# Signing complex gradient sums on TensorE in an S4 channel loop, and moving one copy to VectorE

## The chip, the cores and the metric

The kernel runs on one core of one Trainium2 chip. The metric is the time of one execution in microseconds on the device; the time before is the median of three runs. The engines are TensorE (PE, its weight loads are PEld), VectorE (DVE), ScalarE (ACT), GpSimd (POOL) and SyncE (SP, which issues transfers).

## The reference

The reference is the forward pass and the whole gradient of a gated mix: `out = g * a + (1 - g) * b`, where `a` is multi-head attention over `x` (2048 tokens, 576 channels, 32 heads), `b` an S4 convolution and `g` a sigmoid gate per token. Cut to what this change touches, the S4 part is

```python
dt = exp(log_dt)[:, None];  A = A_re + 1j*A_im;  Bc = B_re + 1j*B_im;  Cc = C_re + 1j*C_im
P = exp((dt*A)[:, :, None] * arange(L))          # 576 channels x 128 states x 2048 steps
K = einsum("dn,dnl,dn->dl", Cc, P, dt*Bc).real   # one filter of 2048 taps per channel
y = irfft(rfft(pad(u)) * rfft(pad(K)))[:L] + u*Dskip
_out, vjp = jax.vjp(forward, ...);  grads = vjp(grad_out)
```

The gradients for `A`, `B`, `C` and `log_dt` need, per channel and state, complex sums over pairs of block states: products (a_r + i a_i)(h_r + i h_i) added up, so that the real part is rr - ii and the imaginary part ri + ir.

## The kernel before

The kernel has a projection stage, then a long attention stage (forward and backward, up to about 2080 us), then the channel loop of the S4 part (up to about 2531 us), and a final stage that forms the outputs. The change lies in the channel loop.

The loop runs over 18 blocks (`NBLK`) of 32 channels (`CB`); the 128 states lie on the partitions. The 2048 tokens are 16 blocks of 128 (`NB`; `NS` = 15). The loop is a software pipeline written out by hand: iteration `i` finishes block `i`, starts the scan of block `i+1`, prepares the inputs of block `i+2` (`sb`) and loads for block `i+3` (`mb`). The order on PE, ACT, DVE and POOL is the order in which the code calls the steps.

The steps of one iteration, with the names that the profile shows:

- `scan`: DVE runs two recurrences in turn, the second half of block `i` and the first half of block `i+1`. Each step is a product `tz` (L733), an addition of `UV` (L736) and an addition into `HG` (L738). `scan_open` (L714) opens a block: it allocates `HG` and copies the first states out of `UV`.
- `rw1` and `rw2`: DVE makes `wab` (L753) and `Rw` (L758) from `HG`.
- `m_sum`, `m_fin`, `m_part`: PE sums `skw` into `misc`, ACT copies into `RX` (L652 to L654); PE makes `psM`, ACT copies it to `mst` (L628), from where it goes to memory.
- `turn_e`: PE transposes `E1n` (1 MB per half block, loaded from memory) into `etp`, ACT copies it to `E1e` (L672). Twice a block.
- `k0`: PE makes 64 matmuls of one column (`misc<-wk,E1n`).
- `uv`: PE multiplies `E1e` and `RX` into `uvp`, ACT scales it into `UV` (L708). Twice a block.
- `t0` and `ybp`: PE adds two products into `yp`, the second from `Rw`; ACT copies `yp` to `yd` (L806).
- `pairs1` and `pairs2`: DVE multiplies `UV` with the casts `hR` and `gR` of `HG` into the bf16 tile `pq` (L812, L841); `psum` lets PE add `pq` over the token blocks with matmuls by the identity into `misc`.
- `m4_copy` (L849): ACT copies the sums from `misc` into the tile `m4` (in the profile `m`), and in the next iteration `sums` (L854, L855) lets POOL subtract and add the four kinds of product into the table `SS`. The last block's `sums` is on DVE.

In a `pq` tile the four kinds of product rr, ri, ir and ii lie side by side, 32 channels each, for every token block. Before, `psum` adds all four in one matmul of 128 columns, 59 matmuls a block (15, 30 and 14 for the three sums). Every matmul has a weight load of its own, also where the weights are the same as before. `etp`, `uvp` and `psM` share four buffers.

Of the kernel before, what the change touches and what calls it, by code (L numbers as in the profile page):

```python
# [9 lines left out]
A = mybir.AluOpType  # L10
ACT = mybir.ActivationFunctionType
BF = mybir.dt.bfloat16
F32 = mybir.dt.float32
# [4 lines left out]
P = 128  # L18


def build(tc, aps, dbg_aps=None, stages=("s1", "attn", "post", "s4", "final")):
    nc = tc.nc
# [6 lines left out]
    def mm(out, lhsT, rhs, start=True, stop=True, **kw):  # L29
        return nc.tensor.matmul(out, lhsT=lhsT, rhs=rhs, start=start, stop=stop, **kw)  # L30
# [31 lines left out]
    with ExitStack() as gctx:  # L62
# [3 lines left out]
        ident_bf = const.tile([P, P], BF, name="ident_bf")  # L66
# [36 lines left out]
        CB = 32  # L103
# [475 lines left out]
        Q = {}  # L579
# [130 lines left out]
        def scan_open(b):  # L710
            B_ = blk(b)
            HG = B_["HG"] = Q["pw"].tile([P, 2, NS, 2, CB], F32, tag="HG", bufs=2, name="HG")
            UVk = B_["UVk"] = B_["UV"][:, :, 0:2 * NB, :].rearrange("p r (s k) c -> p r s k c", s=2)
            (nc.vector.tensor_copy if b == 0 else nc.scalar.copy)(HG[:, :, 0], UVk[:, :, :, 0, :])  # L714

        def scan(*chains):

# [97 lines left out]

        def psum(b, u, pts, n):

            o_ = Q["misc2"][b % 2][:, 4 * u * CB:4 * (u + 1) * CB].rearrange("p (a b c) -> p a b c", a=2, b=2)
            for q, pt_ in enumerate(pts):
                for k in range(n):  # L820
                    mm(o_, lhsT=ident_bf, rhs=pt_[:, :, :, k, :], start=(q == 0 and k == 0),
                       stop=(q == len(pts) - 1 and k == n - 1))

        def pairs1(b):
            B_ = blk(b)
# [16 lines left out]
                                        hR[:, ri, 1:NS, :].unsqueeze(1).to_broadcast([P, 2, NS - 1, CB]), op=A.mult)  # L842
            psum(b, 2, [pD], NS - 1)

        m4s = {}

        def m4_copy(b):
            m4 = m4s[b] = Q["pw"].tile([P, 3, 4, CB], F32, tag="m4", name="m4")
            nc.scalar.copy(m4, Q["misc2"][b % 2][:, 0:12 * CB].rearrange("p (u q c) -> p u q c", u=3, q=4))  # L849

        def sums(b, eng=nc.gpsimd):
            m4 = m4s.pop(b)
            o_ = Q["SS"].rearrange("p (u r) d -> p u r d", r=2)[:, :, :, b * CB:(b + 1) * CB]
            eng.tensor_tensor(o_[:, :, 0], m4[:, :, 0], m4[:, :, 3], op=A.subtract)  # L854
            eng.tensor_tensor(o_[:, :, 1], m4[:, :, 1], m4[:, :, 2], op=A.add)  # L855

        def t0_load(b):
            B_ = blk(b)
# [91 lines left out]
        if "attn" in stages:  # L950
# [5 lines left out]
            with ExitStack() as ctx:  # L956
# [3 lines left out]
                pts = {}  # L960
# [322 lines left out]
                for G in range(NTOT + OFF + 24):  # L1283
# [4 lines left out]
                    if G < NTOT:  # L1288
                        u, s = divmod(G, NST)
                        g, b = units[u]  # L1290
# [11 lines left out]
                    if r1:  # L1302
                        g, b, i, j0 = r1
# [109 lines left out]
        if "s4" in stages:  # L1413
# [8 lines left out]
            with ExitStack() as ctx:  # L1422
# [4 lines left out]
                pps = Q["ps"] = ctx.enter_context(tc.tile_pool(name="s4lps", reuse_waits="tile", bufs=1, space=bass.MemoryType.PSUM))  # L1427
                pidx_i = pc.tile([P, 1], mybir.dt.int32, name="pidx_i")
                nc.gpsimd.iota(pidx_i, pattern=[[0, 1]], base=0, channel_multiplier=1)
                l0col = pc.tile([P, 1], F32, name="l0col")  # L1430
                nc.vector.tensor_copy(l0col, pidx_i)
                l1col = pc.tile([P, 1], F32, name="l1col")
# [17 lines left out]
                with tc.manual_schedule(engines={mybir.EngineType.SP}):  # L1450
                    prep_rx(0, dve_copy)
                    load_en(2, 0, nc.sync.dma_start)
                    wk_cast(0)
                    k0(0)
                    k0_out(0)
                    t0_load(0)
                    turn_e(0, 0, 0, 4, dve_copy)
                    m_sum(0)
                    m_fin(0)
                    uv(0, 0)  # L1460
                    prep_rx(1, dve_copy)
                    load_rx(1, nc.sync.dma_start)
                    turn_e(0, 1, 0, 4, dve_copy)
                    m_part(1)
                    m_skw(1)
                    m_load(2, nc.sync.dma_start)
                    uv(0, 1)
                    turn_e(1, 0, 0, 4, dve_copy)
                    scan_open(0)
                    scan((0, 1, KH, 0), (0, 1, KH, 1))  # L1470
                    turn_e(1, 1, 0, 4)
                    m_sum(1)
                    m_fin(1)
                    load_en(2, 1, nc.sync.dma_start)
                    uv(1, 0)
                    m_part(2)
                    m_skw(2)
                    uv(1, 1)
                    scan_open(1)
                    m_load(3, nc.sync.dma_start)  # L1480
                    prep_rx(2)
                    wk_cast(1)
                    for i in range(NBLK):
                        nx = i + 1 < NBLK
                        mb = i + 3 if i + 3 < NBLK else None
                        sb = i + 2 if i + 2 < NBLK else None
                        if nx:
                            scan((i, KH, NS, None), (i + 1, 1, KH, None))
                        else:
                            scan((i, KH, NS, 0), (i, KH, NS, 1))  # L1490
                        rw1(i)
                        rw2_open(i)
                        rw2(i)
                        if sb is not None:
                            m_sum(sb)
                            m_fin(sb)
                        if mb is not None:
                            m_part(mb)
                            if mb + 1 < NBLK:
                                m_load(mb + 1)  # L1500
                            m_skw(mb)
                        if i > 0:
                            sums(i - 1)
                        if sb is not None:
                            if i % 2 == 1 and (i + 3) // 2 < NBLK // 2:
                                load_par((i + 3) // 2)
                            turn_e(sb, 0, 0, 4)
                        if nx:
                            k0(i + 1)
                        if nx:  # L1510
                            k0_out(i + 1)
                        cast1(i, "hR", 0)
                        nc.scalar.copy(Q["CK"][:, :, :, i * CB:(i + 1) * CB], BK[i]["UV"][:, :, CDK:CDK + 2, :])
                        if sb is not None:
                            uv(sb, 0)
                        t0(i, 0)
                        t0(i, 1)
                        if nx:
                            t0_load(i + 1)
                        cast1(i, "gR", 1)  # L1520
                        if i + 2 >= NBLK:
                            y = 2 * (i + 2 - NBLK)
                            dwq(0, (y, y + 1), "bk", 4)
                            if not nx:
                                dwq_last(0, 1, "bk", 4)
                                load_dq(2)
                        if sb is not None:
                            turn_e(sb, 1, 0, 4)
                        ybp(i, 0)
                        if mb is not None:  # L1530
                            load_en(mb, 0)
                        if sb is not None:
                            uv(sb, 1)
                            scan_open(sb)
                        if i == NBLK - 3:
                            ple_cm.__exit__(None, None, None)
                            Q["nob"] = 2
                            Q["pbw"] = ctx.enter_context(tc.tile_pool(name="pbw0", reuse_waits="tile", bufs=1))
                            r0_cm = tc.tile_pool(name="r0", reuse_waits="tile", bufs=1, side="right")
                            Q["r0"] = r0_cm.__enter__()  # L1540
                            rights.append(r0_cm)
                            load_dq(0)
                        ybp(i, 1)
                        if i == NBLK - 3:
                            load_dq(1)
                        if mb is not None:
                            load_en(mb, 1)
                            prep_rx(mb)
                            if mb % 2 == 1 and mb + 1 < NBLK:
                                load_rx((mb + 1) // 2)  # L1550
                        if mb == NBLK - 1:
                            load_xtok()
                        if sb is None and nx:
                            load_dq(3)
                        yd_out(i, 0)
                        yd_out(i, 1)
                        pairs1(i)
                        pairs2(i)
                        if sb is not None:
                            wk_cast(sb)  # L1560
                        m4_copy(i)
                        if not nx:
                            sums(i, nc.vector)
                        BK.pop(i)

        if "final" in stages and "s4" in stages:
# [304 lines left out]
```

## Time and profile before

| | |
|---|---|
| time before, median of 3 runs | 2687.24 us (2683.43 to 2697.16) |
| the profiled execution's own time | 2685.73 us |
| its span in the profile | 2683.9 us |
| mean granted TensorE clock | 0.968 |
| busy time of PE, DVE, ACT, POOL | 2404.7, 2293.8, 2350.8, 1818.0 us |

Times are microseconds unless marked ns. A busy PE is not PE at its peak, because matmuls overlap and their ends are modelled. From the order of time, the step from one start to the next is the better measure of what a matmul costs in a row of them. "issue" as a releaser means that the engine waited for nothing that the profile shows.

### The profile page before, as it was taken

Reading aid. Unit: us, or ns where it says so; the run is one execution under the profiler, and the core shown is the slowest. Engines: PE = TensorE matmul, PEld = TensorE weight load, DVE = VectorE, ACT = ScalarE, POOL = GpSimd, SP = SyncE. Lnnn points to the kernel's source line nnn. Section 1 sums busy time; section 2 is a strip of 40 time slices with the busy share of each in tenths; the row PEclk is TensorE's granted clock in tenths of the full one; section 3 lists DMA queues with packets and bytes.
Section 4 is the critical chain, followed back from the end, with each engine's and each line's share of the span. In section 5 each row is a group of like instructions: output and inputs, shape, how many; then the busy total and the mean of one; then the engine's idle time right before and its main releaser. Section 6 shows DMA issues by size and latency. Waiting matters only on the chain.

```text
span 2683.9 us, 69949 instructions
## 1 busy us (share of the span) xinstructions
PE 2404.7 (90%) x27411; PEld 1137.9 (42%) x27411; DVE 2293.8 (85%) x4090; ACT 2350.8 (88%) x2744; POOL 1818.0 (68%) x2829
## 2 busy tenths in 40 slices
PE   8799998998899899889888989989887699999999
PEld 4433333333333333333333333333232499998756
DVE  5648999999989999989999989989897589999964
ACT  5489999999999999999999999999995399999221
POOL 0278888888888888888888888887831045555431
PEclk9879999999999999999999999999996699999999
DMA  7637789879979978997898899789679889998895
GB/s 232 196 99 156 154 159 181 167 153 181 172 152 170 183 160 159 178 172 153 165 178 154 161 172 170 153 163 177 143 140 183 191 244 256 259 262 253 261 261 128
DMA packets 1157013, 486.63 MB, mean 181 GB/s; under 512 B 1071061, under 2 KB 1110598, under 8 KB 1154378
## 3 DMA queue, kind: packets, MB, share of 16 engines
q1 hardware_dynamic: 1110650, 341.49, 64.4%
q0 software_dynamic: 44016, 135.16, 18.3%
q10 hardware_dynamic: 2016, 5.51, 0.6%
q8 instruction: 214, 3.51, 0.6%
q14 instruction: 117, 0.96, 0.1%
HBM read 146.27 MB, written 93.80 MB: 89 GB/s over the span
## 4 chain that ended last, share of the span: by engine, by line
ACT 40%; PE 28%; DVE 18%; issue 6%; DMA 4%; POOL 2%; SPq 1%; ACTq 0%; DVEq 0%; POOLq 0%
ACT eb L1387 23%; ACT PT L1382 14%; DVE ds L1392 7%; PE ps_P L30 7%; PE accV L30 2%; PE ps_dx L30 2%; PE turn_p L1095 2%; PE ps_dwq L30 2%; DVE tz L733 2%; PE ps_proj L30 2%; DVE wab L753 2%; PE yp L30 2%; PE accK L30 1%; DVE dvacc L1149 1%; DVE tz L736 1%
## 5 line engine op out<-in xcount | busy, mean ns | idle before, releaser
L1392 DVE TENSOR_TENSOR ds<-ps_P,PT 128x512 bf16<-128x512 f32 x2048 | 1312.3, 683 | 125.5 <-PE ps_P L30 86.8
L1387 ACT ACTIVATE eb<-ps_P 128x1024 bf16<-128x1024 f32 x1024 | 1099.9, 1074 | 34.8 <-PE ps_P L30 34.5
L1382 ACT ACTIVATE PT<-ps_P 128x1024 bf16<-128x1024 f32 x1024 | 1105.0, 1080 | 21.7 <-PE ps_P L30 20.3
L30 PE MATMUL ps_P<-dOaT,VaT_g 32*128 32x512 bf16 x2048 | 581.9, 388 | 31.5 <-DVE ds L1392 16.1
L506 POOL TENSOR_TENSOR et<-eG,eT 128x448 f32<-128x448 f32 x576 | 542.2, 961 | 10.7
L30 PE MATMUL ps_P<-QaT_g,KaT_g 32*128 32x512 bf16 x2048 | 402.9, 386 | 136.5 <-ACT PT L1382 121.8
L30 PE MATMUL ps_P<-KaT_g,QaT_g 32*128 32x512 bf16 x2048 | 406.0, 389 | 1.6 <-ACT eb L1387 0.6
L30 PEld LDWEIGHTS <-KaT_g 32*128 32x128 bf16 x2048 | 147.6, 91 | 467.5 <-issue 451.4
L506 POOL TENSOR_TENSOR Eo<-et,et 128x448 bf16<-128x448 f32 x288 | 327.0, 1135 | 20.8
L30 PEld LDWEIGHTS <-QaT_g 32*128 32x128 bf16 x2048 | 116.1, 91 | 285.3 <-issue 262.4
L30 PE MATMUL accV<-eb,dOa 128*32 128x512 bf16 x2048 | 185.0, 394 | 27.2 <-ACT eb L1387 27.1
L30 PE MATMUL accO<-PT,Vtok_g 128*32 128x512 bf16 x2048 | 207.4, 394 | 0.0
L30 PE MATMUL accK<-dsT,Qtok_g 128*32 128x256 bf16 x4096 | 162.3, 279 | 14.5 <-DMA dsT<-ds 12.4
L30 PE MATMUL accQ<-ds,Ktok_g 128*32 128x512 bf16 x2048 | 161.6, 394 | 2.3 <-DVE dvacc L1149 2.2
L30 PEld LDWEIGHTS <-Vtok_g 128*32 128x32 bf16 x2048 | 52.7, 93 | 222.7 <-issue 222.7
L1100 DVE COPY dsT<-turn_p 128x1024 bf16<-128x1024 bf16 (+1 forms) x216 | 139.2, 644 | 2.1 <-PE turn_p L1095 2.1
L1095 PE MATMUL turn_p<-ident_bf,ds 128*128 128x128 bf16 x1664 | 134.1, 223 | 1.5 <-DVE gb L1167 0.8
L672 ACT COPY E1e<-etp 128x1024 bf16<-128x1024 bf16 x132 | 125.2, 1059 | 2.6 <-PE etp L671 2.6
L506 POOL TENSOR_TENSOR et<-eT 128x32 f32<-128x32 f32 (+3 forms) x288 | 115.9, 422 | 11.4
L1047 POOL TENSOR_TENSOR dOa<-dO_b,rl 128x288 bf16<-128x288 bf16 x32 | 21.5, 673 | 149.9 <-DVE rl L1042 149.9
L30 PEld LDWEIGHTS <-Qtok_g 128*32 128x32 bf16 x4096 | 87.9, 97 | 79.0 <-issue 64.0
L1095 PEld LDWEIGHTS <-ds 128*128 128x128 bf16 x1664 | 97.3, 99 | 49.5 <-issue 49.5
(294 smaller groups left out, 3749.3 us busy)
## 6 DMA issues: line engine op xcount, KB each, us to landing
E_d<-Eo POOLq DMA_DIRECT2D x144, 256.0 KB, 3.4
E1n<-E_d POOLq DMA_DIRECT2D x30, 1024.0 KB, 7.3
T0w<-Kp_d SPq DMA_DIRECT2D x18, 1024.0 KB
xs<-xb_d POOLq DMA_DIRECT2D x28, 512.0 KB, 9.8
dsT<-ds SPq DMA_TRANSPOSE x512
dqkv_d<-dtk POOLq DMA_DIRECT2D x96, 72.0 KB, 4.2
Md_d<-mst SPq DMA_DIRECT2D x18, 288.0 KB
skw<-Md_d SPq DMA_DIRECT2D x72, 64.0 KB
```

Of the source, the lines that this page charges most:

```text
L30: return nc.tensor.matmul(out, lhsT=lhsT, rhs=rhs, start=start, stop=stop, **kw)
L506: nc.gpsimd.tensor_tensor(out, a, b, op=op)
L672: copy(E_[:, 4 * q:4 * q + 4], pt_)
L733: nc.vector.tensor_tensor(tz[x], HG[:, :, k - 1].unsqueeze(1).to_broadcast([P, 2, 2, n, CB]), ZZ.unsqueeze(3).to_broadcast([P, 2, 2, n, CB ...
L736: nc.vector.tensor_tensor(tz[x][:, 0], tz[x][:, 0], UVk[:, :, :, k, :], op=A.add)
L753: nc.vector.tensor_tensor(wab, h_, w_, op=A.mult)
L1095: nc.tensor.transpose(pt_[:, x, qb, :], t_[:, qb * P:(qb + 1) * P], ident_bf)
L1100: (nc.scalar.copy if NTOT <= now[0] < NTOT + OFF else nc.vector.tensor_copy)(o_(), pt_[:, x:x + n])
L1149: nc.vector.tensor_tensor(o_, a_, acc, op=A.add)
L1382: nc.scalar.activation(U["PT"][i, j // 2], ps, ACT.Exp)
L1387: nc.scalar.activation(e, ps, ACT.Exp)
L1392: nc.vector.tensor_tensor(U["ds"][i][:, j, :], ps, U["PT"][i, j // 2][:, j % 2, :], op=A.mult)
```

## The change

`psum` now forms the signed sums on PE. For each sum it makes, in place of each matmul of 128 columns, one of 64 columns by the identity (rr and ri), one of 32 columns by the identity (ir, added to the imaginary part) and one of 32 columns by the negative identity `nident` (ii, subtracted from the real part). `misc` then holds six groups of 32 in place of twelve. `m4_copy` and the two operations of `sums` become one ACT copy of these 192 columns into the table `SS`, at the end of the same iteration. `nident` is made once on DVE before the loop. `scan_open` of block `i+1` is no longer called at the end of the preparation of that block, with the copy on ACT, but at the head of the iteration that scans it, with the copy on DVE. The order of all other instructions on each engine stays.

```diff
         def scan_open(b):
             ...
-            (nc.vector.tensor_copy if b == 0 else nc.scalar.copy)(HG[:, :, 0], UVk[:, :, :, 0, :])
+            nc.vector.tensor_copy(HG[:, :, 0], UVk[:, :, :, 0, :])
...
         def psum(b, u, pts, n):
-            o_ = Q["misc2"][b % 2][:, 4 * u * CB:4 * (u + 1) * CB].rearrange("p (a b c) -> p a b c", a=2, b=2)
-            for q, pt_ in enumerate(pts):
-                for k in range(n):
-                    mm(o_, lhsT=ident_bf, rhs=pt_[:, :, :, k, :], start=(q == 0 and k == 0),
-                       stop=(q == len(pts) - 1 and k == n - 1))
+            o_ = Q["misc2"][b % 2][:, 2 * u * CB:2 * (u + 1) * CB].rearrange("p (r c) -> p r c", r=2)
+            ks = [(q, k) for q in range(len(pts)) for k in range(n)]
+            for q, k in ks:
+                mm(o_, lhsT=ident_bf, rhs=pts[q][:, 0, :, k, :], start=(q == 0 and k == 0), stop=False)
+            for q, k in ks:
+                mm(o_[:, 1], lhsT=ident_bf, rhs=pts[q][:, 1, 0, k, :], start=False, stop=False)
+            for q, k in ks:
+                mm(o_[:, 0], lhsT=Q["nident"], rhs=pts[q][:, 1, 1, k, :], start=False, stop=((q, k) == ks[-1]))
...
-        def m4_copy(b):
-            m4 = m4s[b] = Q["pw"].tile([P, 3, 4, CB], F32, tag="m4", name="m4")
-            nc.scalar.copy(m4, Q["misc2"][b % 2][:, 0:12 * CB].rearrange("p (u q c) -> p u q c", u=3, q=4))
-
-        def sums(b, eng=nc.gpsimd):
-            m4 = m4s.pop(b)
-            o_ = Q["SS"].rearrange("p (u r) d -> p u r d", r=2)[:, :, :, b * CB:(b + 1) * CB]
-            eng.tensor_tensor(o_[:, :, 0], m4[:, :, 0], m4[:, :, 3], op=A.subtract)
-            eng.tensor_tensor(o_[:, :, 1], m4[:, :, 1], m4[:, :, 2], op=A.add)
+        def sums(b):
+            nc.scalar.copy(Q["SS"][:, :, b * CB:(b + 1) * CB], Q["misc2"][b % 2][:, 0:6 * CB].rearrange("p (u c) -> p u c", u=6))
...
+                nident = Q["nident"] = pc.tile([P, P], BF, name="nident")
+                nc.vector.tensor_scalar(nident, ident_bf, -1.0, None, op0=A.mult)
...
                     uv(1, 1)
-                    scan_open(1)
...
                         if nx:
+                            scan_open(i + 1)
                             scan((i, KH, NS, None), (i + 1, 1, KH, None))
...
-                        if i > 0:
-                            sums(i - 1)
...
                             uv(sb, 1)
-                            scan_open(sb)
...
-                        m4_copy(i)
-                        if not nx:
-                            sums(i, nc.vector)
+                        sums(i)
```

More of the change, by code (lines that the diff above doesn't have):

```diff
@@ L843, in pairs2 @@
             psum(b, 2, [pD], NS - 1)
-        m4s = {}
-        def m4_copy(b):
-            m4 = m4s[b] = Q["pw"].tile([P, 3, 4, CB], F32, tag="m4", name="m4")
-            nc.scalar.copy(m4, Q["misc2"][b % 2][:, 0:12 * CB].rearrange("p (u q c) -> p u q c", u=3, q=4))
-        def sums(b, eng=nc.gpsimd):
-            m4 = m4s.pop(b)
-            o_ = Q["SS"].rearrange("p (u r) d -> p u r d", r=2)[:, :, :, b * CB:(b + 1) * CB]
-            eng.tensor_tensor(o_[:, :, 0], m4[:, :, 0], m4[:, :, 3], op=A.subtract)
-            eng.tensor_tensor(o_[:, :, 1], m4[:, :, 1], m4[:, :, 2], op=A.add)
+        def sums(b):
+            nc.scalar.copy(Q["SS"][:, :, b * CB:(b + 1) * CB], Q["misc2"][b % 2][:, 0:6 * CB].rearrange("p (u c) -> p u c", u=6))
         def t0_load(b):
```

## The prediction

> **What bounds the kernel now.** I read in this order: the busy time of the engines in the stretch that the change touches, the chain through it, what each instruction there costs, and the waits. Blocks 1 to 15 of the channel loop run from 2163 to 2484 us; the long DVE product `wab` starts every 21.47 to 22.4 us there, 21.49 in the median. The row of that stretch (its length, busy us of PE, PEld, DVE, ACT and POOL with counts, granted clock, DMA share, GB/s):
>
> ```profile
> 2163.20:2484.00 320.80, 306.97 (x5731) 290.98 (x5729) 316.41 (x731) 299.59 (x474) 172.95 (x131) 1.00 0.89 259
> ```
>
> DVE is busy for 98.6%, PE for 95.7%, ACT for 93.4%. POOL has room at 54%: what is taken from it gains nothing by itself. The chain through one block (start, us, what) shows who hands over to whom:
>
> ```profile
> 2402.15 0.67 DVE tz L733 x2
> ...
> 2410.96 4.36 DVE wab L753
> 2415.34 2.24 DVE Rw L758
> 2417.62 1.87 PE yp L30 x32
> 2419.98 1.36 ACT UV L708 x3
> 2421.43 0.63 ACT UV L708
> 2423.64 0.67 DVE tz L733 x2
> ```
>
> DVE scans and makes `Rw`; PE's `yp` waits for that, then makes `uvp`; ACT turns it into `UV`, which DVE's next scan needs. The `pq` products and the sums over them (`misc<-pq`) hang beside this ring, but the sums stand in PE's order ahead of everything that PE does next. How much PE has left is in the waits (total, times, longest) of 2145 to 2530 us:
>
> ```profile
> PEld L30 <- issue: 17.3, 34, 2.3
> PE yp L30 <- DVE Rw L758: 9.5, 12, 2.2
> DVE tz L733 <- ACT HG L714: 6.3, 5, 3.8
> ```
>
> From start to start, the last matmul before the first `yp<-Rw` and that `yp` stand 0.86 to 1.15 us apart in the nine blocks where no other stall came before, 0.94 in the median; 0.06 is the usual step. (The row's 9.5 us are less, since they count from modelled ends.) So PE's spare time is 0.88 us a block, and its own work 21.49 - 0.88 = 20.61 us.
>
> **The sums on PE.** Their cost is in the order of time (start, us from first start to last end) of one block:
>
> ```profile
> 2215.00 1.75 PE L30 MATMUL misc<-wk,E1n 128*128 128x1 bf16 x64
> 2222.96 1.87 PE L30 MATMUL yp<-Rw,E1n 128*128 128x30 bf16 x32
> 2224.65 1.97 PE L30 MATMUL uvp<-RX,E1e 128*128 128x64 bf16 x32
> 2228.13 3.47 PE L30 MATMUL misc<-pq,ident_bf 128*128 128x128 bf16 x59
> ```
>
> Without the last one's own 0.16 to 0.25 us, the steps are 25, 53, 56 and 56 ns. Now 59 matmuls of 128 columns take 59 x 56 = 3.30 us. The change makes 59 of 64 columns and 118 of 32, each with its own weight load. Contiguous matmuls elsewhere in the trace step 56 ns at 128 columns, 122.5 at 288 and 216 at 512, a line of 0.417 ns a column and 2.7 ns: 64 columns give 29.3. By the line 32 columns would give 16, but the row with one column and a full 128x128 load per matmul steps 25, so I take 25. Sum: 59 x 29.3 + 118 x 25 = 4.68 us, 1.38 more a block. At least it is 177 x 25 = 4.43 (1.13 more). At most it is the 53 to 56 ns of `yp` and `uvp`, 177 x 55 = 9.7 (6.4 more); these have as few columns, but write them at a stride, 8 or 16 elements apart, which the sums do not; I stay with the row of one column and the line.
>
> [...]
>
> The extra 1.38 goes first into the 0.88 of spare time; 0.50 a block stays.
>
> **Fetching PE's program.** The waits called "issue" have a pattern that this change touches:
>
> ```profile
> q8 instruction: 214, 3.51, 0.6%
> 2221.41 1.44 PE L671 MATMUL etp<-ident_bf,E1n 128*128 128x128 bf16 x23 [0.56 <-issue]
> ```
>
> PE has 27411 loads and as many matmuls, 54822 instructions; 214 packets of 16.4 KB make 256 instructions each. Numbered in order, PE stood still in mid-group at 2157.5, 2179.2, 2221.4, 2264.8 and 2306.9 us, for 0.5 to 1.5 us, and these places are exact multiples of 256 instructions apart. In all five the wait ended 1.4 to 1.5 us after a packet of this queue ended. The packet of the next piece ends 1.3 to 5.7 us, in the median 3.1, after PE passes such a border, so the next piece is there after about 4.6 us (2.7 to 7.2). Today 256 instructions last 5.3 us where the fast one-column matmuls are, and 7.5 in the median, and the five stalls all follow those fast matmuls.
>
> The sums become 354 instructions in 4.68 us: 256 of them last 3.4 us, 1.2 less than the 4.6. They span 1.4 pieces a block, so up to 1.7 us a block of new standing still; pieces that only partly lie in the sums pay less, others arrive late and pay more. I take 1.4, between 0 (all early) and 5.3 a block (all as late as the latest, 7.2 - 3.4 = 3.8 a piece).
>
> [...]
>
> **DVE.** `scan_open` moves to DVE, ahead of the scan in the same iteration: one copy per block that lasted 0.218 us in block 0 and steps some 0.14. It waits for ACT's last `UV`, and behind it stand the scans of both blocks, where now the older block's first product runs while ACT copies. From ACT's queue goes the copy of 0.298 us. Against that the POOL sums end: `wab` took 4.34 to 4.36 us beside them and 4.153 and 4.159 in the two blocks without, `Rw` 2.23 against 2.16. So DVE gets -0.26 + 0.14, about 0.1 less work; I count nothing, since PE is later. The matrix `nident` is made once, before the loop, where DVE is mostly idle.
>
> **ACT.** The copy of 384 columns (0.50 us) becomes one of 192, between the 0.23 of 32 columns and 0.50: 0.36. With the `HG` copy ACT loses 0.4 us. The new `sums` copy waits for the end of PE's sums, as the old one did; behind it are the `RX` copies, `mst` and the `E1e` copies that free PE's buffers. ACT idles 1.0 us before `mst` today (21.3 us of such waits in the loop), so its later start is PE's delay over again, not an addition.
>
> **POOL.** It loses two operations of 1.6 and 4.3 us a block; behind them in its queue stand the loads `par` and `E1n` and the store `yd`. Those wait for PE to release buffers (80.3 us of waits for `E1n`), so they hardly start sooner. SP's order does not change.
>
> **The end of the loop.** The sums of blocks 16 and 17 lie on the chain as they are:
>
> ```profile
> 2509.32 3.30 PE misc L30 x59
> ...
> 2526.97 3.30 PE misc L30 x59
> ```
>
> They pay all 1.38, with 0.7 for the fetch: 4.2 together. Block 15's sums fall under the 9.78 us load of `dq`. The DVE sums of the last block (two of 0.25) go, but PE's 29.6 us of `ps_dwq` end later and set the end.
>
> **The sum.** 15 blocks x (0.50 + 1.4) = 28.5, and 4.2: 33 us. The profiled execution took 2685.73 us, 2683.9 of it the span and 1.8 around it; 1.5 below the median of 2687.24. From the profile 2719, from the median 2720.
>
> **Rivals.**
> *The fetch keeps up.* Then 15 x 0.50 + 2 x 1.38 = 10 us: 2697, the same within measurement (0.5%, 13.4 us, is about what a measurement of this kernel can tell). For it: today only five pieces of 47 stop PE. Against: none of today's 256 instructions ran in 3.4 us.
> *Short matmuls step like `yp`.* 15 x (6.4 - 0.88) + 2 x 6.4 = 96: 2783. Against it: the one-column row.
> *Not slower: DVE is the true bound, and PE's additions hide.* The place is the `yp` that waits for `Rw`. If the 177 matmuls took under 3.30 + 0.88 = 4.18 us (23.6 ns each), PE would still wait there, and the ring would follow DVE, 0.1 us shorter: 15 x 0.1 = 2 us less, 2685. For it: DVE's 98.6% and the 6.3 us waited for `HG`. Against it: no full 128x128 matmul of this stretch steps under 25 ns.
>
> **How the numbers follow.** The forecast has 0.64, the fetch that keeps up 0.20, the slow steps 0.08, DVE's bound 0.05; 0.03 is left for a gain that I can't name. The low end, 2693, is the second case with the 25 ns floor (15 x 0.25 + 2 x 1.13 = 6); the high end, 2764, is the forecast with three quarters of the fetch's upper bound, 3.9 a block (15 x 4.4 + 2 x 5.3 = 77). That leaves out the slow steps and DVE's bound. Faster by over 0.5%: 0.03, within 0.20, slower 0.77.
>
> **What would show it.** Right: `misc<-pq` as 177 matmuls in some 4.7 us with gaps called issue inside or just after; `wab` every 23 to 24 us; no wait of `yp` for `Rw`; DVE waiting for `UV`; `wab` at 4.16. Wrong: a step of over 40 ns, a period under 22, or PE still waiting for `Rw`.

## The result and the profile after

The changed kernel takes 2731.49 us (median of 4, 2727.35 to 2737.35), beside 2689.34 for the kernel before in the same session: ratio 1.016, 95% interval 1.0139 to 1.0182, so 37 to 49 us slower. Measured again later, beside other experiments, it took 2721.31 against 2687.03: 1.0137 (1.0112 to 1.0162), 30 to 44 us. The forecast was 2720, 33 us slower.

The profiled execution took 2737.35 us, with a span of 2735.6, 51.7 more than before. Of these, 9.1 us have nothing to do with the change: the last `ds` of the attention stage ends at 2093.7 us instead of 2084.6, and in the other kernels profiled here, whose attention code is the same, it ends anywhere from 2081.7 to 2092.9. From `wab` of block 1 to that of block 15 it is 337.8 us instead of 302.5, 35.3 more; the rest is 1.7 us at the start of the loop and 5.7 after block 15.

First the row of the steady stretch (length, busy us of PE, PEld, DVE, ACT, POOL, granted clock, DMA share, GB/s):

```profile
2174.00:2520.00 346.00, 329.92 (x7309) 311.74 (x7306) 304.97 (x735) 285.52 (x446) 82.14 (x101) 0.95 0.79 234
```

DVE fell from 98.6% to 88.1%, ACT from 93.4% to 82.5%, POOL from 54% to 24%; PE stays at 95.4%. The granted clock is 0.95, where it was 1.00. A block now takes 24.13 us (23.2 to 25.3) instead of 21.61, both as a mean of blocks 1 to 14. The chain through one block:

```profile
2317.11 1.69 PE yp L30 x32
2318.80 5.44 PE misc L30 x184
2324.24 1.44 issue
2325.68 0.38 PE misc L30
2326.06 2.05 PE psM L30 x30
```

It no longer goes through `wab` and `Rw` on DVE. It stays on PE, through the sums (177 and the first 7 of the next 8 matmuls into `misc`), and through time in which PE waited for nothing that the profile shows. The waits (total, times, longest, 2145 to 2580 us) say the same:

```profile
DVE HG L714 <- ACT UV L708: 54.0, 17, 9.6
PEld L30 <- issue: 24.0, 36, 2.0
ACT SS L849 <- PE misc L30: 23.3, 17, 6.1
PE misc L30 <- issue: 13.7, 11, 1.9
```

The wait of `yp` for `Rw` is gone; DVE waits for `UV`, and ACT waits for the sums. This is one block's sums, in order of time on PE:

```profile
2246.15 0.98 PE L30 MATMUL misc<-pq,ident_bf 128*128 128x64 bf16 x30
2246.98 0.53 PE L30 MATMUL misc<-pq,nident 128*128 128x32 bf16 x15
2247.36 1.78 PE L30 MATMUL misc<-pq,ident_bf 128*128 128x64 bf16 x60
2248.98 0.90 PE L30 MATMUL misc<-pq,nident 128*128 128x32 bf16 x30
2249.73 0.91 PE L30 MATMUL misc<-pq,ident_bf 128*128 128x64 bf16 x28
2250.49 0.25 PE L30 MATMUL misc<-pq,nident 128*128 128x32 bf16 x4
2252.66 0.40 PE L30 MATMUL misc<-pq,nident 128*128 128x32 bf16 x10 [1.92 <-issue]
```

From start to start the matmuls of 64 columns step 29 ns and both kinds of 32 columns 25 ns. After 167 of the 177, PE stands still for 1.92 us inside a run of equal instructions. There is one such stop in every block from 1 to 14, at an exact multiple of 256 PE instructions from the last, and it begins in the sums or in the few matmuls after them; block 14 has a second one, 256 instructions later, in `misc<-wk`. All 15 ended 1.3 to 1.6 us after a packet of the queue that the profile calls instruction (`q8`) had ended, as the five stops of the kernel before did after 1.4 to 1.5 us. Together they are 1.43 us a block (1.27 in the second profile of the same kernel, where some blocks have two). What else answers to the prediction:

```profile
q8 instruction: 231, 3.78, 0.6%
L753 DVE TENSOR_TENSOR wab<-HG,par x18: 4144/4152/4161, 2155.8 to 2563.8; 128x3840 f32<-128x3840 f32 x18
```

The program of PE is 17 packets longer (4248 instructions), and `wab` (ns: least, median, most) is at 4.15 us in every block, as it was before in the two blocks without POOL's operations beside it (4.153 and 4.159). At the end of the loop the sums stand bare on the chain:

```profile
2557.09 4.04 PE misc L30 x152
2561.13 1.86 issue
2562.99 0.79 PE misc L30 x25
...
2578.95 4.66 PE misc L30 x177
```

### The profile page after: what moved, and what is told of

Read it like the earlier page. It is cut to its first block, busy times and chain, and to the rows that moved or that the text cites. A ratio compares the mean times of both kernels' runs of the same rounds, so it can differ in the third digit from the quotient of the medians.

```text
span 2735.6 us, 74195 instructions
## 1 busy us (share of the span) xinstructions
PE 2451.2 (90%) x29535; PEld 1176.5 (43%) x29535; DVE 2292.8 (84%) x4106; ACT 2347.2 (86%) x2727; POOL 1719.1 (63%) x2795
## 4 chain that ended last, share of the span: by engine, by line
ACT 38%; PE 37%; DVE 12%; issue 6%; DMA 3%; POOL 2%; SPq 1%; ACTq 0%; DVEq 0%; POOLq 0%
ACT eb L1381 22%; ACT PT L1376 14%; DVE ds L1386 7%; PE ps_P L30 7%; PE misc L30 5%; PE yp L30 3%; PE accV L30 2%; PE etp L671 2%; PE turn_p L1089 2%; PE uvp L30 2%; PE ps_dx L30 2%; PE ps_dwq L30 2%; PE accK L30 2%; PE psM L30 1%; DVE dvacc L1143 1%
## 5 line engine op out<-in xcount | busy, mean ns | idle before, releaser
L689 POOL DMA_DIRECT2D E1n<-E_d x30 | 23.0, 765 | 163.2 <-PE yp L30 133.8
L1089 PEld LDWEIGHTS <-ds 128*128 128x128 bf16 x1664 | 98.6, 100 | 50.4 <-issue 50.4
```

The lines of the kernel that those rows point to most:

```text
L689: dma(En[:, x * n:(x + 1) * n].rearrange("p (g c) r n -> p g (c r n)", c=EQ), E_d[:, (dG + x * n) // EQ:(dG + (x + 1) * n) // EQ, 0:EQ * 2 ...
L1089: nc.tensor.transpose(pt_[:, x, qb, :], t_[:, qb * P:(qb + 1) * P], ident_bf)
```

## The experiments

Theory R: the loss is on PE, in two parts, the longer array time and the stops while PE's program is fetched. Rivals: M, the moved copy or the ACT copy that waits for the sums lengthens the ring; A, the array time alone does it, and the stops are harmless.

**One part alone.**

```diff
e1_old_sums, against the changed kernel: psum as before
+            o_ = Q["misc2"][b % 2][:, 4 * u * CB:4 * (u + 1) * CB].rearrange("p (a b c) -> p a b c", a=2, b=2)
+            ...  mm(o_, lhsT=ident_bf, rhs=pt_[:, :, :, k, :], ...)
e2_only_pe, against the kernel before: psum of the changed kernel, all by ident_bf
+            nc.scalar.copy(m4 ..., Q["misc2"][b % 2][:, 0:6 * CB].unsqueeze(1).to_broadcast([P, 2, 6 * CB]))
```

> The changed kernel with the 59 sums of 128 columns of before; the one ACT copy takes the first 192 of the 384 columns, so the signing is left out. Theory R (the loss is the longer time on PE and the stops while its program is fetched): with PE back at 3.30 us a block, the loop follows DVE, which lost the contention with POOL (0.26 us) and gained a copy (0.14): 0 to 4 us under the kernel before, wab every 21.3 to 21.5 us. Theory M (the moved copy on DVE or the ACT copy that waits for the sums makes the ring longer): most of the loss stays, 15 us or more over the kernel before.

Measured: 2684.88 against 2688.48, ratio 0.9983 (0.9959 to 1.0007). The block takes 21.50 us. Everything in the change but the short matmuls costs nothing that this measurement shows, at least while PE is on time. M falls for that case; the place of the copy with a late PE is asked below.

> The kernel before with only the 177 short matmuls in place of the 59 (all by the identity; the m4 copy keeps its 384 columns by reading the 192 twice, so the values of the sums are left out); POOL sums and the copy on ACT stay. Theory R: the whole loss is here, 35 to 45 us over the kernel before, one stop of 0.7 to 2.1 us a block in or just after the sums. Theory M: under 20 us over the kernel before.

Measured: 2719.1 against the same 2688.48, 1.0115 (1.0091 to 1.0139), 24 to 37 us; the block 23.56 us, with stops of 1.17 us. That is less than R expected, and 12 us under the first measurement of the whole change, but inside the interval of its second (30 to 44). The short matmuls carry the loss.

**Array time and number of instructions apart.** These two decide between R and A.

```diff
e3_wide59, against the changed kernel
+            w_ = 192 if u == 0 else 182
+            o_ = Q["misc2"][b % 2][:, 0:w_]
+            ...  mm(o_, lhsT=ident_bf, rhs=fl[:, min(k, 8) * CB:min(k, 8) * CB + w_], ...)   # one per token block, 59 in all
e4_132short, against the changed kernel
+            ks = [(q, k, x) for q in range(len(pts)) for k in range(n) for x in range(4)][:(33, 66, 33)[u]]
+            ...  mm(o_[:, y % 2], lhsT=ident_bf, rhs=pts[q][:, x // 2, x % 2, k, :], ...)
```

> The changed kernel with 59 matmuls of 182 or 192 columns in place of the 177: 15 x 82.7 + 44 x 78.6 ns = 4.70 us on PE, the time of the 177 matmuls, in the 118 instructions of before (the values of the sums are left out). Theory R: the array time stays, the stops for the program go: 15 x 0.5 + 3 = 8 to 12 us over the kernel before, wab every 22.0 us. Rival A (the array time alone makes the loss, through the ring of PE, ACT and DVE): 35 to 45 us over the kernel before, wab every 24 us.

Measured: 2696.9, 1.0037 (1.0019 to 1.0056), 8 us. The row of blocks 1 to 14:

```profile
2181.30:2495.00 313.70, 311.45 (x5481) 296.20 (x5482) 296.51 (x701) 279.46 (x438) 77.44 (x95) 0.99 0.86 250
```

PE is busy for 99.3%, a block takes 22.41 us, and the stops are 0.09 us a block. The same array time in a third of the instructions costs 8 us in place of 34 to 42: A falls.

> The changed kernel with 132 matmuls of 32 columns in place of the 177: 132 x 25 ns = 3.30 us on PE, the time of the 59 of before, in 264 instructions (part of the products is left out of the sums). Theory R: the array time is as before, a stop of about 1 us a block comes, of which PE's spare 0.9 us takes most: 2 to 12 us over the kernel before, stops called issue in or after the sums in most blocks. Rival A: no loss, 0 to 4 us under the kernel before.

Measured: 2703.33, 1.0063 (1.0038 to 1.0088), 15 us, 3 more than the upper end for R; A, which expected no loss, falls again. The array time is 3.30 us, and the block takes 22.40 us, 0.9 more than with the 59 matmuls of e1; the stops are 0.90 us a block, in most blocks. PE's spare time did not take them up as I expected: the wait for `Rw` fell only from 0.56 (in e1) to 0.28 us. The granted clock over these blocks is 0.96, where it is 0.99 in e1, so part of the 0.9 can be the clock.

**The order of the sums.**

```diff
e5_spread, against the changed kernel: where psum stands in PE's order
                             uv(sb, 1)
+                        pairs1(i)
...
+                        pairs2(i)              # with psum 1; psum 2 and the copy of the sums come
+                        if i > 0:              # in the next iteration, behind m_part
+                            psum2(i - 1)
```

> The changed kernel with the same 177 matmuls in another place of PE's order: the first 45 between uvp and the second yp, the next 90 after it, the last 42 behind psM of the next block (the copy of the sums follows them). Same instructions, same array time. Theory R: 256 instructions now last 4.2 us at least where they lasted 3.4, so the stops fall from 1.43 to 0.3 to 0.8 us a block: 10 to 18 us under the changed kernel, 22 to 32 over the kernel before, wab every 22.8 to 23.5 us. Rival A (the stops don't depend on how fast the instructions run, or the rest of the loss is another wait): within 5 us of the changed kernel.

Measured: 2719.82, 1.0113 (1.0088 to 1.0138). That is 30 us over the kernel before in the same session, inside the 22 to 32 of R; the changed kernel stood 42 and 34 us over its own. Against the first time of the changed kernel it is 12 us less, against the second 1.5, so the time settles nothing. The stops fell from 1.43 and 1.27 to 0.93 us a block, not to 0.3 to 0.8, and moved: in front of `misc<-wk` and `uvp`; the last 42 short matmuls now run shortly before the 64 one-column ones. The block took 23.47 us.

**The place of the copy.**

```diff
e6_copy_on_act and e10_copy_on_act_again, against the changed kernel
-                            scan_open(i + 1)
...
                             uv(sb, 1)
+                            scan_open(sb)          # on nc.scalar, as before
e8_copy_on_dve, against the kernel before: the reverse
```

> The changed kernel with the first states' copy on ScalarE again, at its old place. Asks for the 12 us by which the short matmuls alone (31 us over the kernel before) fall short of the whole change (42). Theory R: PE is the bound, so this place of the copy costs nothing: within 4 us of the changed kernel. Theory M: the copy on DVE, which waits for ACT's last UV ahead of both scans, costs 0.3 us a block or more once PE is late: 5 to 12 us under the changed kernel.

> The changed kernel itself, beside the next one on the same chip, since the 9 us between the changed kernel and the one with the copy back on ScalarE came from two chips and lie inside their intervals. Theory R (place of the copy costs nothing while PE is the bound): the two within 4 us of each other, stops for the program 1.2 to 1.5 us a block in both. Theory M (the copy on DVE costs once PE is late): 5 to 12 us above the next one, a period longer by 0.3 us a block or more.

> The changed kernel with the first states' copy on ScalarE at its old place, beside the changed kernel on the same chip. Theory R: within 4 us of it. Theory M: 5 to 12 us under it.

e6 took 2722.44 (1.013, 1.0098 to 1.0161), which looked like 9 us for the copy. Side by side the two are the other way round: 2721.31 (1.0137) for the changed kernel, 2726.67 (1.0151, 1.0124 to 1.0177) with the copy on ACT. They are 5 us apart, a little more than the 4 that R allowed, but not in the direction of M, and their intervals overlap. A cost of the copy on DVE is not to be seen, and a difference of some 10 us between measurements on two chips should not be given a cause.

> The kernel before with only the first states' copy moved to DVE at the head of the iteration. Theory R: DVE is full there, so the copy of 0.14 us a block is paid less the 0.1 us that DVE waited for ACT's copy: 0 to 3 us over the kernel before. Theory M: 5 us or more over.

Measured: 2692.01 against 2690.3, 1.001 (0.9992 to 1.0028): no difference, as R expected.

**POOL and DVE.**

```diff
e7_pool_early, against the kernel before
+                        if i > 0:
+                            sums(i - 1)
                         if mb is not None:
                             m_part(mb)
                             ...
-                        if i > 0:
-                            sums(i - 1)
```

> The kernel before with the two POOL sums ahead of m_load in POOL's order instead of behind it; nothing left out. Before, the second one ran beside DVE's wab and Rw, which took 4.345 and 2.23 us instead of 4.155 and 2.16. [...]

Measured: 2695.69 against 2690.3, 1.0025 (1.0009 to 1.0042): slower. My estimate was a gain of 2 to 4 us, from the 0.26 us a block by which `wab` and `Rw` are longer in the kernel before with the second operation beside them: a miss. POOL's operations in this kernel (ns: least, median, most):

```profile
L854 POOL TENSOR_TENSOR SS<-m x17: 497/3562/5716, 2170.7 to 2525.2; 128x96 f32<-128x96 f32 x17
L855 POOL TENSOR_TENSOR SS<-m x17: 390/4294/4307, 2174.5 to 2525.7; 128x96 f32<-128x96 f32 x17
```

Beside the scan the first takes 3.56 us, where it took 1.63 in the kernel before, so the second runs beside `wab` as ever, and `wab` is at 4.36. The order of time shows why an earlier start did not help: in 16 of 17 blocks the first one ended only after `wab` had begun, however early it started.

```profile
2279.53 3.24 POOL L854 TENSOR_TENSOR SS<-m 128x96 f32<-128x96 f32 x1
...
2282.42 4.38 DVE L753 TENSOR_TENSOR wab<-HG,par 128x3840 f32<-128x3840 f32 x1
...
2282.74 4.30 POOL L855 TENSOR_TENSOR SS<-m 128x96 f32<-128x96 f32 x1
```

The loads of `m_load` behind them start only after both, and what these loads bring ends up, by way of `psM` and `mst`, in `skw`. PE waited three times for `skw`, 6.4 us in all (in the kernel before once, 0.4), shortly before the two longest blocks, of 27.8 and 25.0 us, where 21.5 is usual. That this is the loss fits, but no run shows it.

**A version that beats both.** e1 showed that the change without its short matmuls is no slower than before. So the 59 sums stay, and PE signs only their result. The ACT copy rounds the sums to bf16 on the way.

```diff
e11_sign3, against the kernel before
-            nc.scalar.copy(m4, ...)                                   # f32
+            nc.scalar.copy(m4.rearrange("p u a b c -> p (u a b c)"), Q["misc2"][b % 2][:, 0:12 * CB])   # bf16
...
+            mm(o_, lhsT=ident_bf, rhs=m4[:, :, 0], start=True, stop=False)
+            mm(o_[:, :, 1], lhsT=ident_bf, rhs=m4[:, :, 1, 0], start=False, stop=False)
+            mm(o_[:, :, 0], lhsT=Q["nident"], rhs=m4[:, :, 1, 1], start=False, stop=True)
+            ...  nc.scalar.copy(Q["SS"][:, :, b * CB:(b + 1) * CB], ...)
```

> A version meant to keep the good part of the change: the kernel before with its 59 sums of 128 columns, the ACT copy now to bf16, and in the next block three matmuls (192, 96 and 96 columns, 0.17 us, 6 instructions) that add and sign by the identity and the negative identity, then one ACT copy of 192 columns into the table; POOL does no sums. Theory R: PE still has spare time, few instructions come in, DVE gains the 0.26 us a block that POOL's sums cost wab and Rw: 1 to 5 us under the kernel before, wab every 21.3 to 21.6 us and 4.15 us long. Rival: ACT, with one more copy of 0.36 us a block, takes the gain: 0 to 6 us over the kernel before.

Measured: 2684.73 against 2691.67, ratio 0.9978 (0.9963 to 0.9993), 2 to 10 us faster than before.

```profile
2174.00:2476.00 302.00, 296.38 (x5557) 280.72 (x5554) 297.87 (x696) 288.22 (x469) 77.76 (x96) 1.00 0.90 262
```

DVE is at 98.6% again, the clock at 1.00; the block takes 21.34 us and `wab` 4.15. PE keeps 0.49 us of spare time a block in front of `yp`, and the stops are at most 0.08.

## Why the prediction was right, and where it was off

**Sums on PE.** Right to the nanosecond: 29 and 25 ns a step, 4.68 us without a stop. The row of one-column matmuls and the line through longer ones were the right neighbours; the matmuls of 32 columns step 25 ns with a load in each. One load lasts 96 ns in the mean, but the loads overlap, since 826 of them together were under way for only 23.8 us:

```profile
L30 PEld LDWEIGHTS <-nident 128*128 128x128 bf16 x826 | 23.8, 96 | 2.9 <-issue 2.9
```

**Spare time.** Too large. The prediction let 0.88 us of the added 1.38 vanish and 0.50 stay. With the fetch out of the way (e3) a block takes 0.80 more than before and 0.91 more than e1, which has everything else of the change. The 0.88 came from the nine blocks that no other stall shortened; over blocks 1 to 14 the mean is 0.67.

**Fetching the program.** Right in kind, since the stops stand at multiples of 256 instructions, and in size by some luck: 1.4 us a block predicted, 1.43 and 1.27 measured. The 1.4 was picked from a range of 0 to 5.3, and its working had 1.4 short pieces a block at up to 1.2 us each; the trace has 15 stops in 14 blocks, of 0.7 to 2.1 us, so fewer and longer ones. e3 and e4 show that it is the number of instructions in a short time that matters, not the array time: with 118 instructions in 4.7 us the stops are 0.09 us, with 264 in 3.3 us 0.90, with 354 in 4.7 us 1.27 to 1.43. That the fetch keeps up, the second case, is refuted.

**What was missing.** 20.61 and 1.38 and 1.43 make 23.42 us a block; the profile has 24.13, and 23.78 in the second one, where the stops are 1.27. Of the 0.5 to 0.7 that remain, about 0.3 are the spare time again: in e3, with the same array time and almost no stops, the median block took 22.26 us, where the sum had 20.61 + 1.38 = 21.99. The other 0.44 and 0.25 are a term that the sum did not have. The granted clock is low after some of the stops, 0.50 in the rows of one block:

```profile
2376.06 1.61 PE L30 MATMUL psM<-xs,gyp 128*32 128x128 bf16 x23 [1.34 <-issue]
2377.60 2.84 PE L671 MATMUL etp<-ident_bf,E1n 128*128 128x128 bf16 x32
...
2376.06:2379.48 3.42, 3.42 (x41) 2.79 (x41) 3.42 (x11) 1.34 (x2) 1.48 (x3) 0.50 0.32 48
```

The 32 `etp` that took 1.95 to 1.98 us at a granted clock of 1.00 take 2.84. Ten such stretches of 3.41 us lie between 2181 and 2475 us, and six in the same blocks of the second profile; in the kernel before there is none from 2148 to 2482. e3 has one, in the block with its only stop: that block took 23.97 us, 1.71 over the median, and the stop accounts for 1.27 of it. An estimate from this, 0.44 us a stretch, makes 0.31 and 0.19 us a block. That the clock is the missing term is so worked out from three profiles, not shown by a run of its own.

**DVE, ACT, POOL.** As predicted: DVE gained (`wab` 4.15, `Rw` 2.16) and waits for `UV` all the same, 2.76 us a block; the place of the copy added nothing that can be seen (e1, e9 with e10). ACT's longer wait for the sums was not tested by itself; the short matmuls alone (e2) cost nearly what the whole change did, 31 us against 42 and 34. POOL's free time bought nothing to be seen in the changed kernel.

**The end of the loop.** 4.2 us predicted, 5.7 measured from the `wab` of block 15 on, and 6.8 in the second profile.

**The sum.** 33 us predicted, 42 and 34 measured. A block took 2.52 and 2.17 us more than before, where the sum had 1.90: the spare time was 0.3 to 0.4 us a block too large and the clock was left out. That the second measurement lies within 2 us of the forecast is in part luck. The chances did not add up either: by the list of cases the slower ones make 0.72 and those within the measurement 0.25, since DVE's bound, 2 us less, belongs there; the 0.77 counted its 0.05 as slower. The case of the short matmuls at 53 to 56 ns is refuted by the 25 and 29; that DVE is the true bound is refuted by its waits for `UV`.

## What to carry to other kernels

Price a matmul twice, as array time and as an instruction: here the same 4.7 us of PE work cost 8 us in 59 matmuls and 34 to 42 in 177. Where an engine stands still at multiples of a number of its instructions, as PE did here at multiples of 256, count how long that many last at the new pace (here 3.4 us) and compare it with the time from one such border to the arrival of the next piece (here about 4.6 us, an estimate from the trace of before). And apply an operation such as a sign to the result of a reduction, not to each of its terms: three matmuls a block did what 118 had done.

## What was not expected of the hardware

- In the changed kernel PE's granted clock is 0.50 for ten stretches of 3.41 us between 2181 and 2475 us. They begin inside a stop or up to 2.8 us after one, and these stops lasted 0.9 to 2.1 us from start to start, in a loop where PE was busy for 95.4%. The short sums are not needed for it: e3 has none, and has such a stretch at 2233.0 us, after its one stop of 1.3 us. Such a stop is not enough either: the kernel before stopped for up to 1.5 us between 2157 and 2307 us and has no such stretch there. What decides is open.
- The end of POOL's two operations on 96 columns went by where DVE was, not by their own start. In the kernel before, 16 of 17 times, the first one (L854) ended 0.32 to 0.34 us after `wab` began, whether it had started 0.7 or 5.4 us ahead of `wab`, and the second (L855) ended 0.24 to 0.26 us after `wab` ended. In e7 it was so again, 0.33 to 0.36 and 0.24 to 0.26 us. Only in the last of these blocks, beside a scan of operations half as large, did the two take 0.42 and 0.39 us; there the rows of two DVE operations beside them took 0.56 and 0.71 us, where 0.35 and 0.48 are usual. `wab` took 4.345 us in the median with the second one beside it and 4.153 and 4.159 without, 0.2 less; the second one took 4.30 us in the median and 0.39 in that last block, so POOL lost far more than DVE. In e2 some of these operations took 0.42 us beside `wab` as well; what decides is open.
